# First networks of two tiles side by side, an output product with wide moving operands, and a narrowing without GpSimd

## The chip, the cores and the metric

The kernel runs on one core of one Trainium2 chip. The metric is the device time of one execution in microseconds; three runs of the kernel before gave 1218.34, 1219.1 and 1219.85 us.

## What is computed

For 6016 tokens and 256 channels, a channel attention is followed by two feed-forward networks. Weights come as 64-bit floats and the kernel rounds them to 32 bits itself ("narrowing").

```python
qn, kn = q / norm(q over tokens), k / norm(k over tokens)
a   = softmax(kn.T @ qn / tau)              # 256 x 256
x   = v @ a                                 # 6016 x 256
h   = x @ w_in                              # 2048 wide
g   = h where h >= 1, 0 where h <= -1, (h + 1)**2 / 4 between
y   = g @ w_out                             # first network
xn  = y / sqrt(mean(y*y) + 1e-6) * rms_g
out = (silu(xn @ w_gate) * (xn @ w_val)) @ w_out2   # second network, 1536 wide
```

## The kernel before, in words

Tokens are handled in 12 tiles: eleven of 512 and one of 384. Channels or hidden units lie on the partitions and tokens on the free axis, so that a matmul has a 128x128 stationary block of weights and a moving block of up to 512 tokens. Every product is made from two parts of each operand, a high part rounded to the fp32r format and the remainder: high x high, low x high and high x low, so three matmuls for one. `split` (L88) makes the parts: a copy on ScalarE (L89) and a subtraction (L86), on VectorE or, where an engine is given, on GpSimd.

**Start.** q and k are loaded in 14 chunks (L306 to L336). ScalarE squares them (L320), VectorE sums the squares (L325), TensorE accumulates the 256x256 scores (L298). Norms, softmax and a transpose give `at`, the attention in two parts. It is folded into the first weight: `make_w1` (L411) multiplies a 512-column group of w_in with it, giving w1 in two parts, `w1h` and `w1l`.

**Narrowing.** 34 jobs of 128x512 words narrow the weights. A job loads 512 KB into one of three `wide` buffers (L143) and works in place (`narrow`, L155): VectorE clamps the high words (L158), shifts the three top bits of the low words down (L162), takes the sign bit over (L166); ScalarE scales the exponent (L170); VectorE shifts and joins (L174); ScalarE rounds the high part (L180); GpSimd subtracts (L182). Then the buffer is free for SP's next load. `pump` (L212) moves each of at most two jobs in flight one step on and starts a new one; it is called once for each item of the order, and `require` (L221) calls it until the named weights are ready.

**First network** (A and B). Item ("1", t, f) multiplies w1's block f with tile t's v (`emit_A`, L432, 6 matmuls), makes g (L449, L450 on ScalarE, L451 on VectorE) and splits it (L461: the subtraction is GpSimd's for t < 2 or f < 3). Three items later `emit_B` (L464, 6 matmuls) adds block f's part to the sum y, which has a PSUM buffer of two banks of its own (`ps_y`). After block 15, `norm` (L479) makes the second network's input in five steps on VectorE, ScalarE, GpSimd (the power, L506) and TensorE.

**Second network** (GV and D). Item ("2", t, f) multiplies gate and value block f (`emit_GV`, 12 matmuls), makes u (L552, L553), splits it, and two items later `emit_D` (L564) adds block f's part to the output. There the tokens are the stationary operand, 128 at a time, and the 256 columns of w_out2 move: 12 matmuls of 256 columns in a tile of 512. The output accumulates in a PSUM buffer of its own (`ps_o`), tokens on the partitions; `store` (L580) copies one half on ScalarE (L588) and one on VectorE (L590) and sends each with one DMA of SP.

**Order.** A list written by hand (L597 to L620) holds 16 items of the first network for each tile and, between them, the 12 items of the second network of the tile before, of which six are left for the next tile's time. The scheduler orders the instructions of each engine by a simulated timeline, starting from the order in which they are written. All loads and stores stand on SP's queue.

Of the kernel before, what the change touches and what calls it, by code (L numbers as in the profile page):

```python
# [17 lines left out]
SKEW = 6  # L18
LAG = 12
MID = 8  # L20
# [3 lines left out]
PRE = 2  # L24
# [5 lines left out]
QK_CHUNKS = (2, 2, 4, 4, 4, 4, 4, 4, 4, 4, 4, 3, 2, 2)  # L30

# [4 lines left out]
def tile_channel_attention_two_ffn(  # L36
# [36 lines left out]
    ps_y = ctx.enter_context(tc.tile_pool(name="ps_y", bufs=1, space=bass.MemoryType.PSUM))  # L73
    ps_o = ctx.enter_context(tc.tile_pool(name="ps_o", bufs=1, space=bass.MemoryType.PSUM))

    def mm_tile(name):
        return ps_mm.tile([P, TOK], F32, tag="mm", name=name)

# [76 lines left out]
    def narrow(x, hi, lo):  # L155
# [26 lines left out]
        nc.gpsimd.tensor_tensor(out=lo, in0=got, in1=hi.bitcast(F32), op=ALU.subtract)  # L182
# [4 lines left out]

    later = []
# [5 lines left out]
    def narrow_job():  # L194
        if not wide:
            fetch()
        key, x, dst = wide.pop(0)
        if w1_done[0] >= 0:
            while jobs and len(wide) < STAGE - FLIGHT:
                fetch()  # L200
        hi, lo = dst()
        yield from narrow(x, hi, lo)
        ready.add(key)

    flight = []
    w1_done = [-1]

    def may_start():
        key = wide[0][0] if wide else jobs[0][0] if jobs else None
        return key is not None and not (key[0] == "wi" and key[1] > w1_done[0] + 2)  # L210

    def pump():  # L212
# [33 lines left out]
    def wi_jobs(todo, g):  # L246
        for c in range(NC):
            todo.append((("wi", g, c), (w_in, c * P, 1), g * TOK, wi_dst(g, c)))
# [8 lines left out]
    for g in range(2):  # L257
        wi_jobs(jobs, g)
    wo_jobs(0)
    for g in range(2, NG):  # L260
        wi_jobs(later, g)
        wo_jobs(g - 1)
    wo_jobs(NG - 1)
    w2 = {}
    for g in range(F2 // TOK):
# [20 lines left out]
    s_ps = [  # L286
        ps_y.tile([P, 2, TOK], F32, tag="y", name="s_ps0")[:, 0, :C],
        ps_o.tile([P, 2, 2, C], F32, tag="o", name="s_ps1")[:, 0, 0, :],
    ]
# [47 lines left out]
    for _ in range(PRE):  # L337
        fetch()
# [72 lines left out]
    def make_w1(g, b):  # L411
        h, l = wi[g]
        ah, al = at[b]
        ps = mm_tile(f"w1_ps{g}_{b}")
        i = 0
        for c in range(NC):
            sl = slice(c * P, (c + 1) * P)
            for x, w in ((ah, h), (ah, l), (al, h)):
                nc.tensor.matmul(ps, x[:, sl], w[:, c, :], start=(i == 0), stop=(i == 3 * NC - 1))
                i += 1  # L420
        sl = slice(g * TOK, (g + 1) * TOK)
        split(w1h[:, b, sl], w1l[:, b, sl], ps)
# [33 lines left out]
    def finish_g(t, f):  # L456
# [281 lines left out]
```

## Time and profile before

| what | value |
|---|---|
| median of 3 runs | 1219.1 us (1218.34 to 1219.85) |
| profiled execution | 1220.48 us, span 1218.7 us |
| TensorE busy | 1179.0 us, 97% of the span, 6000 matmuls |
| VectorE busy | 678.5 us, 56% |
| ScalarE busy | 638.3 us, 52% |
| GpSimd busy | 179.8 us, 15% |
| DMA | 43.48 MB, 36 GB/s over the span |

Busy times of engines overlap. A matmul's duration in the profile is longer than the distance to the next one, since matmuls are pipelined; what one costs in a row of them is read from start to start. The idle time of an engine that does not bound the kernel costs nothing. PE is TensorE, DVE VectorE, ACT ScalarE, POOL GpSimd, SPq the queue of SyncE.

### The profile page before, as it was taken

Reading aid. Unit: us, or ns where it says so; the run is one execution under the profiler, and the core shown is the slowest. Engines: PE = TensorE matmul, PEld = TensorE weight load, DVE = VectorE, ACT = ScalarE, POOL = GpSimd, SP = SyncE. Lnnn points to the kernel's source line nnn. Section 1 sums busy time; section 2 is a strip of 40 time slices with the busy share of each in tenths; the row PEclk is TensorE's granted clock in tenths of the full one; section 3 lists DMA queues with packets and bytes.
Section 4 is the critical chain, followed back from the end, with each engine's and each line's share of the span. In section 5 each row is a group of like instructions: output and inputs, shape, how many; then the busy total and the mean of one; then the engine's idle time right before and its main releaser. Section 6 shows DMA issues by size and latency. Waiting matters only on the chain.

```text
span 1218.7 us, 15601 instructions
## 1 busy us (share of the span) xinstructions
PE 1179.0 (97%) x6000; PEld 1010.6 (83%) x6000; DVE 678.5 (56%) x977; ACT 638.3 (52%) x1076; POOL 179.8 (15%) x128
## 2 busy tenths in 40 slices
PE   7888789999999999999999999999999999999998
PEld 6666567888888888888888888888888888899998
DVE  5899999464464464364365355355355345445443
ACT  6566776454464455454455455455445445445432
POOL 0255775110010010010010010010010010010000
PEclk9999899999999999999999999999999999999999
DMA  9734433010001001001001001001001000000000
GB/s 352 191 103 121 116 94 85 1 18 18 1 7 29 1 1 35 1 1 35 1 1 36 1 1 35 1 1 35 1 1 31 1 1 18 1 1 18 1 18 14
DMA packets 67275, 43.48 MB, mean 36 GB/s; under 512 B 51456, under 2 KB 57472, under 8 KB 67200
## 3 DMA queue, kind: packets, MB, share of 16 engines
q1 hardware_dynamic: 67200, 42.48, 12.4%
q8 instruction: 47, 0.77, 0.3%
q14 instruction: 28, 0.23, 0.1%
HBM read 36.31 MB, written 6.16 MB: 35 GB/s over the span
## 4 chain that ended last, share of the span: by engine, by line
PE 84%; DVE 7%; DMA 4%; issue 2%; ACT 1%; SPq 1%; POOL 0%; DVEq 0%; POOLq 0%; ACTq 0%
PE y L471 18%; PE h L439 18%; PE o L573 16%; PE vp L541 15%; PE gp L541 15%; DMA qk<-in_q_dram 2%; DVE wide L162 1%; DVE wide L174 1%; DVE wide L158 1%; DVE wide L166 1%; DVE g L451 1%; DMA wide<-in_moe_w_in_dram 1%; SPq L124 1%; DMA wide<-in_moe_w_out_dram 0%; DMA wide<-in_moe_w_val_dram 0%
## 5 line engine op out<-in xcount | busy, mean ns | idle before, releaser
L89 ACT ACTIVATE uh<-u 128x512 fp32r<-128x512 f32 (+1 forms) x144 | 89.8, 624 | 256.1 <-PE o L573 252.4
L86 POOL TENSOR_TENSOR gl<-g,gh 128x512 fp32r<-128x512 f32 (+1 forms) x62 | 85.6, 1384 | 833.0 <-ACT gh L89 619.8
L451 DVE SCALAR_TENSOR_TENSOR g<-h,g 128x512 f32<-128x512 f32 (+1 forms) x192 | 129.6, 676 | 121.6 <-ACT g L450 121.6
L86 DVE TENSOR_TENSOR ul<-u,uh 128x512 fp32r<-128x512 f32 (+1 forms) x144 | 99.2, 689 | 158.5 <-ACT uh L89 158.0
L553 DVE TENSOR_TENSOR u<-u,vp 128x512 f32<-128x512 f32 (+1 forms) x144 | 97.3, 676 | 136.2 <-PE vp L541 133.7
L89 ACT ACTIVATE gh<-g 128x512 fp32r<-128x512 f32 (+1 forms) x192 | 119.0, 620 | 91.6 <-DVE g L451 90.0
L449 ACT ACTIVATE g<-h 128x512 f32<-128x512 f32 (+1 forms) x192 | 112.5, 586 | 93.7 <-PE h L439 92.5
L573 PE MATMUL o<-wdh,ul 128*128 128x256 f32 x564 | 159.6, 283 | 0.0
L573 PE MATMUL o<-wdl,uh 128*128 128x256 f32 x564 | 159.5, 283 | 0.0
L573 PE MATMUL o<-wdh,uh 128*128 128x256 f32 x564 | 158.8, 282 | 0.0
L439 PE MATMUL h<-vh,w1h 128*128 128x512 f32 (+1 forms) x384 | 150.1, 391 | 8.1 <-DVE g L451 7.8
L471 PE MATMUL y<-gh,woh 128*128 128x512 f32 (+1 forms) x384 | 149.7, 390 | 5.4 <-DVE x L485 4.7
L471 PE MATMUL y<-gl,woh 128*128 128x512 f32 (+1 forms) x384 | 149.8, 390 | 1.9 <-POOL gl L86 1.9
L439 PE MATMUL h<-vh,w1l 128*128 128x512 f32 (+1 forms) x384 | 149.3, 389 | 0.0
L471 PE MATMUL y<-gh,wol 128*128 128x512 f32 (+1 forms) x384 | 149.2, 389 | 0.0
L439 PE MATMUL h<-vl,w1h 128*128 128x512 f32 (+1 forms) x384 | 148.3, 386 | 0.0
L86 DVE TENSOR_TENSOR gl<-g,gh 128x512 fp32r<-128x512 f32 (+1 forms) x130 | 91.1, 701 | 76.5 <-ACT gh L89 75.2
L450 ACT ACTIVATE g<-g 128x512 f32<-128x512 f32 (+1 forms) x192 | 119.0, 620 | 4.4
L541 PE MATMUL gp<-xh,wgh 128*128 128x512 f32 (+1 forms) x288 | 111.7, 388 | 3.8 <-DVE g L451 3.6
L541 PE MATMUL vp<-xh,wvh 128*128 128x512 f32 (+1 forms) x288 | 111.2, 386 | 1.6 <-ACT u L552 1.6
L573 PEld LDWEIGHTS o<-wdl,uh 128*128 128x128 f32 x564 | 107.6, 191 | 5.1
L573 PEld LDWEIGHTS o<-wdh,uh 128*128 128x128 f32 x564 | 107.5, 191 | 5.0
(109 smaller groups left out, 2053.3 us busy)
## 6 DMA issues: line engine op xcount, KB each, us to landing
wide<-in_moe_w_out_dram SPq DMA_DIRECT2D x14, 512.0 KB, 3.7
out_dram<-ob SPq DMA_DIRECT2D x23, 256.0 KB, 2.2
vin<-in_v_dram SPq DMA_DIRECT2D x88, 64.0 KB, 2.5
qk<-in_q_dram SPq DMA_DIRECT2D x9, 512.0 KB, 10.2
qk<-in_k_dram SPq DMA_DIRECT2D x9, 512.0 KB, 10.2
wide<-in_moe_w_in_dram SPq DMA_DIRECT2D x8, 512.0 KB, 4.6
wide<-in_moe_w_gate_dram SPq DMA_DIRECT2D x6, 512.0 KB, 3.6
wide<-in_moe_w_val_dram SPq DMA_DIRECT2D x6, 512.0 KB, 3.6
```

The source lines that it names most:

```text
L86: (eng or nc.vector).tensor_tensor(out=dst_lo, in0=src, in1=hi.bitcast(F32), op=ALU.subtract)
L89: nc.scalar.activation(out=dst_hi, in_=src, func=AF.Copy)
L124: nc.sync.dma_start(out=xv[32 * a:32 * a + 32, c, :n // 32, :], in_=src[a, c])
L158: nc.vector.tensor_scalar(out=high.bitcast(F32), in0=high.bitcast(F32), scalar1=WIDE_MAX, scalar2=-WIDE_MAX, op0=ALU.min, op1=ALU.max,)
L439: nc.tensor.matmul(ps[:, :n], w[:, c, f * P:(f + 1) * P], x[:, c, :n], start=(i == 0), stop=(i == 3 * NC - 1),)
L449: nc.scalar.activation(out=r[:, :n], in_=ps[:, :n], func=AF.Relu, bias=0.5, scale=0.5)
L450: nc.scalar.activation(out=r[:, :n], in_=r[:, :n], func=AF.Square)
L451: nc.vector.scalar_tensor_tensor(out=r[:, :n], in0=ps[:, :n], scalar=1.0, in1=r[:, :n], op0=ALU.max, op1=ALU.min)
L471: nc.tensor.matmul(y_ps[t][:, c, :n], w[:, f, c * P:(c + 1) * P], x[:, :n], start=(f == 0 and i == 0), stop=(f == NF1 - 1 and i == 2),)
L541: nc.tensor.matmul(ps[:, :n], w[:, c, f * P:(f + 1) * P], x[:, c, :n], start=(i == 0), stop=(i == 3 * NC - 1),)
L553: nc.vector.tensor_tensor(out=u[:, :n], in0=u[:, :n], in1=ps[1][:, :n], op=ALU.mult)
L573: nc.tensor.matmul(o_ps[t][:, b // 2, b % 2, :], x[:, sl], w[:, f, :], start=(f == 0 and i == 0 and b % 2 == 0), stop=(f == NF2 - 1 and i ...
```

## The change

- The order is new. The first networks of tiles 0 and 1 run side by side, with tile 1's 16 blocks spread from place 1.5 to 19 along tile 0's; then the first network of tile t has the second network of tile t - 2 beside it. The first four blocks of tile 2 stand alone, and four blocks of tile 0's second network are left for tile 3's time. 24 blocks of the second network follow the last first-network block, where there were 18.
- `y` and the output share two PSUM buffers of two banks (`ps_yo`) in turn.
- `emit_D` makes the weights stationary and the tokens moving, as in B: 6 matmuls of 512 columns for a tile of 512. The output then has channels on the partitions; `store` turns 32x32 blocks on VectorE and sends them with eight DMAs of 64 KB. The last tile keeps the old form.
- In `narrow`, ScalarE makes the low words' three bits by a scaled copy in place of VectorE's shift, and VectorE makes the last subtraction in place of GpSimd.
- g's subtraction is on GpSimd only for t > 3 and f < 3, and the narrowings of w_in write straight to where w1 will stand.
- Ten pumps run beside the q/k chunks 7 to 11 (`PUMPS`); the two loads ahead of time (`PRE`) are gone. A pump is called for every item and a second one for every third.

```diff
-SKEW = 6
-LAG = 12
-MID = 8
+
+
+PAIR = (1.5, 19.0)
+ALONE = 4
+HELD = 4
 BLAG = 3
 W1_AT = (0, 4, 8)
 STAGE = 3
-PRE = 2
...
+PUMPS = (0, 0, 0, 0, 0, 0, 0, 2, 2, 2, 2, 2, 0, 0)
+
+LOW_BITS = 0.9365 * 2.0 ** -29
...
-    ps_y = ctx.enter_context(tc.tile_pool(name="ps_y", bufs=1, space=bass.MemoryType.PSUM))
-    ps_o = ctx.enter_context(tc.tile_pool(name="ps_o", bufs=1, space=bass.MemoryType.PSUM))
+    ps_yo = ctx.enter_context(tc.tile_pool(name="ps_yo", bufs=2, space=bass.MemoryType.PSUM))
...
-        nc.vector.tensor_scalar(
-            out=low, in0=low, scalar1=29, scalar2=None, op0=ALU.logical_shift_right
-        )
+        nc.scalar.activation(out=low, in_=low, func=AF.Copy, scale=LOW_BITS)
         yield
...
-        nc.gpsimd.tensor_tensor(out=lo, in0=got, in1=hi.bitcast(F32), op=ALU.subtract)
+        sub_hi(lo, got, hi)
...
+    wi = {0: [opp.tile([P, NC, TOK], F32R, tag="op", name=f"wi{i}") for i in range(2)]}
+    for g in range(1, F1 // TOK):
+        wi[g] = [w[:, :, g * TOK:(g + 1) * TOK] for w in (w1h, w1l)]
...
+        for _ in range(PUMPS[ci]):
+            pump()
...
-    def make_w1(g, b):
-        h, l = wi[g]
-        ah, al = at[b]
-        ps = mm_tile(f"w1_ps{g}_{b}")
-        i = 0
-        for c in range(NC):
-            sl = slice(c * P, (c + 1) * P)
-            for x, w in ((ah, h), (ah, l), (al, h)):
-                nc.tensor.matmul(ps, x[:, sl], w[:, c, :], start=(i == 0), stop=(i == 3 * NC - 1))
-                i += 1
+    def make_w1(g):
+        require(*[("wi", g, c) for c in range(NC)])
+        h, l = wi.pop(g)
+        got = []
+        for b in range(NC):
+            ah, al = at[b]
+            ps = mm_tile(f"w1_ps{g}_{b}")
+            i = 0
+            for c in range(NC):
+                sl = slice(c * P, (c + 1) * P)
+                for x, w in ((ah, h), (ah, l), (al, h)):
+                    nc.tensor.matmul(
+                        ps, x[:, sl], w[:, c, :], start=(i == 0), stop=(i == 3 * NC - 1)
+                    )
+                    i += 1
+            got.append(ps)
         sl = slice(g * TOK, (g + 1) * TOK)
-        split(w1h[:, b, sl], w1l[:, b, sl], ps)
-        if b == NC - 1:
-            w1_done[0] = g
-            del wi[g]
+        for b in range(NC):
+            split(w1h[:, b, sl], w1l[:, b, sl], got[b])
...
-        split(gh[:, :n], gl[:, :n], r[:, :n], nc.gpsimd if t < 2 or f < 3 else nc.vector)
+        split(gh[:, :n], gl[:, :n], r[:, :n], nc.gpsimd if t > 3 and f < 3 else nc.vector)
...
-            y_ps[t] = ps_y.tile([P, 2, TOK], F32, tag="y", name=f"y{t}")
+            y_ps[t] = yo_tile(f"y{t}")
...
+            o_ps[t] = yo_tile(f"o{t}")
         uh, ul = u_op.pop((t, f))
         wdh, wdl = w2["dh"], w2["dl"]
-        for b in range(n // P):
-            sl = slice(b * P, (b + 1) * P)
-            for i, (x, w) in enumerate(((uh, wdh), (uh, wdl), (ul, wdh))):
+        if t == NT - 1:
+
+            for b in range(n // P):
+                sl = slice(b * P, (b + 1) * P)
+                o = o_ps[t][:, b // 2, (b % 2) * C:(b % 2 + 1) * C]
+                for i, (x, w) in enumerate(((uh, wdh), (uh, wdl), (ul, wdh))):
+                    nc.tensor.matmul(
+                        o, x[:, sl], w[:, f, :],
+                        start=(f == 0 and i == 0 and b % 2 == 0),
+                        stop=(f == NF2 - 1 and i == 2),
+                        skip_group_check=True,
+                    )
+            return
+        for c in range(NC):
+            sl = slice(c * P, (c + 1) * P)
+            for i, (w, x) in enumerate(((wdh, uh), (wdl, uh), (wdh, ul))):
                 nc.tensor.matmul(
-                    o_ps[t][:, b // 2, b % 2, :], x[:, sl], w[:, f, :],
-                    start=(f == 0 and i == 0 and b % 2 == 0),
-                    stop=(f == NF2 - 1 and i == 2),
-                    skip_group_check=True,
+                    o_ps[t][:, c, :n], w[:, f, sl], x[:, :n],
+                    start=(f == 0 and i == 0), stop=(f == NF2 - 1 and i == 2),
...
+        if t < NT - 1:
+            dst = out[n0:n0 + n, :].rearrange("(b j) (c a i) -> a c j b i", j=32, c=NC, a=4, i=32)
+            for c in range(NC):
+                ob = tmp_tile(f"ob{t}_{c}")
+                nc.vector.transpose(out=ob[:, :n], in_=o[:, c, :n])
+                src = ob.rearrange("p (b i) -> p b i", i=32)
+                for a in range(4):
+                    nc.sync.dma_start(out=dst[a, c], in_=src[32 * a:32 * a + 32, :n // 32, :])
+            return
...
+    at_block = [((f, 0), ("1", 0, f)) for f in range(NF1)]
+    for f in range(NF1):
+        at_block.append(((PAIR[0] + f * (PAIR[1] - PAIR[0]) / (NF1 - 1), 1), ("1", 1, f)))
+    order = [block for _, block in sorted(at_block)]
+
+    second = [("2", t, f) for t in range(NT) for f in range(NF2)]
+    done = 0
+    for t in range(2, NT):
+        first = ALONE if t == 2 else 0
+        n = NF2 - HELD if t == 2 else NF2 + HELD if t == 3 else NF2
+        base = done
         for f in range(NF1):
             order.append(("1", t, f))
-            if f < mid:
-                keep = len(early) * (mid - 1 - f) // mid
-                if early:
-                    keep = min(keep, SKEW * (mid - 1 - f) // mid)
-                while len(early) > keep:
-                    order.append(early.pop(0))
-            else:
-                keep = (NF2 - SKEW) * (NF1 - 1 - f) // (NF1 - mid)
-                while len(late) > keep:
-                    order.append(late.pop(0))
-    order.append(("flush1",))
-    order += m2
-    order += [("2", NT - 1, f) for f in range(NF2)]
+            while done < base + n * (f + 1 - first) // (NF1 - first):
+                order.append(second[done])
+                done += 1
+    order += [("B",)] * BLAG
+    order += second[done:]
...
+        work(1)
+        pump()
+        if i % 3 == 0:
             pump()
```

## Rows read from the trace of the kernel before

**Rows 1.** Windows of three stretches: length, busy us (instructions) by engine, PEclk, DMA share, GB/s.

```profile
64.60:204.20 139.60, 115.77 (x471) 88.42 (x470) 136.57 (x173) 98.31 (x172) 89.63 (x60) 0.95 0.40 111
204.20:1214.70 1010.50, 1010.48 (x5308) 877.85 (x5307) 495.93 (x747) 501.14 (x853) 81.61 (x57) 1.00 0.05 11
257.19:351.37 94.18, 94.18 (x483) 80.67 (x483) 46.60 (x70) 47.85 (x81) 7.32 (x5) 1.00 0.05 12
```

**Rows 2.** Timeline of TensorE from 500 us: start us, duration us, line, operation.

```profile
500.40 0.28 PE L573 MATMUL o<-wdh,uh 128*128 128x256 f32 x1
...
501.83 0.40 PE L439 MATMUL h<-vh,w1h 128*128 128x512 f32 x1
...
503.22 0.39 PE L471 MATMUL y<-gh,woh 128*128 128x512 f32 x1
...
504.58 0.39 PE L541 MATMUL gp<-xh,wgh 128*128 128x512 f32 x1
```

**Rows 3.** Groups of TensorE from 64.6 to 204.2 us: count, busy us, mean ns.

```profile
L573 PE MATMUL o<-wdl,uh 128*128 128x256 f32 x9 | 2.5, 283 | 0.0
L573 PE MATMUL o<-wdh,uh 128*128 128x256 f32 x9 | 2.5, 282 | 0.0
L573 PE MATMUL o<-wdh,ul 128*128 128x256 f32 x8 | 2.3, 283 | 0.0
```

**Rows 4.** Groups of VectorE in the same stretch.

```profile
L166 DVE SCALAR_TENSOR_TENSOR wide<-wide 128x512 uint32<-128x512 uint32 x28 | 29.5, 1053 | 0.2
L174 DVE SCALAR_TENSOR_TENSOR wide<-wide 128x512 uint32<-128x512 uint32 x28 | 28.0, 1002 | 0.7 <-ACT wide L170 0.6
L162 DVE TENSOR_SCALAR wide<-wide 128x512 uint32<-128x512 uint32 x27 | 22.3, 827 | 0.0
L158 DVE TENSOR_SCALAR wide<-wide 128x512 f32<-128x512 f32 x27 | 21.9, 813 | 2.1 <-DMA wide<-in_moe_w_in_dram 0.9 <-DMA wide<-in_moe_w_out_dram 0.6 <-DMA wide<-in_moe_w_val_dram 0.5
L451 DVE SCALAR_TENSOR_TENSOR g<-h,g 128x512 f32<-128x512 f32 x31 | 20.7, 676 | 0.0
```

**Rows 5.** Timeline of all engines from 85 us: start us, duration us.

```profile
86.49 0.68 DVE L451 SCALAR_TENSOR_TENSOR g<-h,g 128x512 f32<-128x512 f32 x1
...
87.09 0.68 DVE L166 SCALAR_TENSOR_TENSOR wide<-wide 128x512 uint32<-128x512 uint32 x1
...
90.94 1.50 POOL L182 TENSOR_TENSOR wol<-wide,woh 128x512 fp32r<-128x512 f32 x1
...
91.18 1.53 DVE L162 TENSOR_SCALAR wide<-wide 128x512 uint32<-128x512 uint32 x1
...
93.96 0.42 DVE L158 TENSOR_SCALAR wide<-wide 128x512 f32<-128x512 f32 x1
...
94.30 0.42 DVE L162 TENSOR_SCALAR wide<-wide 128x512 uint32<-128x512 uint32 x1
...
94.63 0.69 DVE L86 TENSOR_TENSOR w1l<-w_ps,w1h 128x512 fp32r<-128x512 f32 x1
```

**Rows 6.** Groups of VectorE in the whole span: count, busy us, mean ns.

```profile
L325 DVE TENSOR_TENSOR acc<-acc,sq 128x2048 f32<-128x2048 f32 x9 | 20.6, 2293 | 13.4 <-ACT sq L320 13.4
...
L500 DVE STREAM_TRANSPOSE sb<-ms 128x512 f32<-128x512 f32 x11 | 7.8, 706 | 1.3 <-PE ms L499 1.3
...
L590 DVE COPY ob<-o 128x512 f32<-128x512 f32 x11 | 7.5, 685 | 0.0
```

**Rows 7.** Timeline of ScalarE, five instructions in a row from 153.28 us.

```profile
153.28 0.58 ACT L449 ACTIVATE g<-h 128x512 f32<-128x512 f32 x1
153.76 0.66 ACT L170 ACTIVATE wide<-wide 128x512 f32<-128x512 f32 x1
...
155.41 0.57 ACT L449 ACTIVATE g<-h 128x512 f32<-128x512 f32 x1
```

**Rows 8.** Timeline of SP's queue at the end of the q/k stage.

```profile
28.15 8.82 SPq L124 DMA_DIRECT2D vin<-in_v_dram  x5
37.08 0.42 SPq L310 DMA_DIRECT2D qk<-in_q_dram  x1
```

More of the change, by code (lines that the diff above doesn't have):

```diff
@@ L186, in tile_channel_attention_two_ffn @@
     ready = set()
-    later = []
     def fetch():
@@ L197, in narrow_job @@
         key, x, dst = wide.pop(0)
-        if w1_done[0] >= 0:
-            while jobs and len(wide) < STAGE - FLIGHT:
-                fetch()
+        while jobs and len(wide) < STAGE - FLIGHT:
+            fetch()
         hi, lo = dst()
@@ L215, in pump @@
                 flight.remove(job)
-        if len(flight) < FLIGHT and may_start():
+        if len(flight) < FLIGHT and (wide or jobs):
             job = narrow_job()
@@ L256, in tile_channel_attention_two_ffn @@
     NG = F1 // TOK
[L257 to L263, printed above, removed]
+    later = []
+    for g in range(NG):
+        wi_jobs(g)
+        wo_jobs(g)
     w2 = {}
@@ L285, in tile_channel_attention_two_ffn @@
     acc = sp.tile([P, 2, JM, C], F32, name="acc")
[L286 to L289, printed above, removed]
+    s_ps = [yo_tile(f"s_ps{b}")[:, 0, :C] for b in range(NC)]
     NQ = len(QK_CHUNKS)
@@ L630, in work, with finish_all_g, next_B @@
                 tasks.remove(task)
[L632 to L637 removed]
+                n_norms[0] = max(0, n_norms[0] - 1)
     m1, m2 = [], []
+    def finish_all_g():
+        for key in list(g_f32):
+            finish_g(*key)
     def step1(t, f):
         if t == 0 and f in W1_AT:
[L642 to L645 removed]
+            make_w1(W1_AT.index(f) + 1)
         ps = emit_A(t, f)
         m1.append((t, f))
[L648 to L649 removed]
+        finish_all_g()
         start_g(t, f, ps)
         if len(m1) > BLAG:
[L652 to L654 removed]
+            next_B()
+    def next_B():
+        t, f = m1.pop(0)
+        if (t, f) in g_f32:
+            finish_all_g()
         if t == 0:
@@ L658, in did_B @@
         if f == NF1 - 1:
-            tasks.insert(0, norm(t))
+            n_norms[0] += 1
+            tasks.insert(n_norms[0] - 1, norm(t))
     def step2(t, f):
@@ L677, in did_D @@
             store(t)
-    for it in order:
+    jobs.extend(later)
+    for _ in v0:
+        pass
+    make_w1(0)
+    for i, it in enumerate(order):
         if it[0] == "1":
             _, t, f = it
-            if f == 0 and t + 1 < NT:
+            if t == 0 and f == 1:
+                load_v(1)
+                for _ in prep_v(1):
+                    pass
+            if t > 0 and f == 0 and t + 1 < NT:
                 load_v(t + 1)
-            if f == 8 and t + 1 < NT:
+            if t > 0 and f == 8 and t + 1 < NT:
                 tasks.append(prep_v(t + 1))
             step1(t, f)
-            work(1)
-            pump()
         elif it[0] == "2":
@@ L692, in tile_channel_attention_two_ffn @@
             step2(*it[1:])
-            work(1)
-            pump()
-        else:
-            finish_g(*m1[-1])
-            for i in range(BLAG, 0, -1):
-                did_B(*m1[-i])
-            work(2)
+        else:
+            next_B()
+        work(1)
+        pump()
+        if i % 3 == 0:
+            pump()
     finish_u(*m2[-1])
```

48 lines of the change are left out of this document (9 added, 39 removed).

## The prediction, made blind

> **What bounds the kernel now.** I read the stretches first [rows 1]. From 204.2 us to 1214.7 us TensorE is busy for 1010.48 of 1010.50 us at full granted clock, with VectorE and ScalarE at half load: here only less TensorE work can shorten the time. One tile takes 94.18 us there, again without a gap. The stretch before it, from the first matmul of tile 0's first network (64.6 us) to 204.2 us, looks different: VectorE is busy 136.57 of 139.6 us, ScalarE 98.31, and TensorE holds only 471 matmuls. So there are two questions: what do the second part's matmuls cost, and what does VectorE do in the first.
>
> For the matmuls the timeline of TensorE by single instructions serves, read from start to start, since the durations overlap [rows 2]. Twelve 256-column matmuls of emit_D take 501.83 - 500.40 = 1.43 us, 0.119 each. Six 512-column ones of emit_B take 504.58 - 503.22 = 1.36 us, 0.2267 each. Twice 0.119 is 0.238, so a split matmul costs about 12 ns more than a whole one of the same columns. The six of emit_A that stand right behind emit_D take 1.39 us, 0.2317 each: 0.03 us per block more.
>
> In the stretch at the start, 26 of the 471 matmuls are those short ones [rows 3]; the work is 445 x 0.2267 + 26 x 0.119 = 104.0 us, and 139.6 - 104.0 = 35.6 us are lost. The cause is VectorE: the four narrowing groups (L158, L162, L166, L174) make 101.7 of its 136.57 us [rows 4]. In the timeline [rows 5] L162 runs 1.53 us while GpSimd's subtraction of 1.50 us runs, and 0.42 us when none does; L162 and L166 have means of 0.827 and 1.053 us against 0.42 and 0.68 for single free ones. GpSimd's subtractions stretch VectorE. Free instructions start 0.60 us apart (86.49 to 87.09) and the two of 0.42 us 0.34 apart (93.96, 94.30, 94.63).
>
> **The change, part by part.** The sum is made against the profiled execution: 1220.48 us, span 1218.7. The median of three runs is 1219.1, 1.4 us below; I take the differences from the median.
>
> *emit_D with 512 columns.* For 11 of 12 tiles, six matmuls take the place of twelve in each of 132 blocks. A whole tile then has 96 + 96 + 144 + 72 + 2 = 410 matmuls of 512 columns, 410 x 0.2267 = 92.95 us, against 94.18 [rows 1]: 1.23 us, in 11 tiles 13.5 us. Of this 0.03 x 132 = 4.0 us is the slower pitch behind emit_D; if it stays, 9.5. I take 13.5, since emit_D becomes like emit_B, behind which the pitch is 0.2267; it is all on the path, as nothing hides TensorE there. Ends: 9.5 and 13.5.
> The Trainium skill (TensorE: Matmul & The Clock Gate, Back-to-back issue gap) gives a lone warm matmul N/2.4 + 2.5 ns, so a removed matmul of the same total columns would save 2.5 ns; 792 of them give an estimate of 2.0 us. The rows here show 0.119 and 0.2267 us where that formula has 0.109 and 0.216, and I go by the rows.
>
> *The store.* Two 32x32-block transposes on VectorE take the place of a ScalarE copy and a VectorE copy (0.685 us); from PSUM such a transpose takes 0.706 [rows 6]. That is 0.73 us more per tile on an engine busy 46.60 of 94.18 us [rows 1]: free. Eight DMAs of 64 KB stand on SP's queue instead of two, in front of later v loads, which have a tile's time. The last tile keeps the old form, so the end is as now. The output buffer is free only after both transposes, and the sum of one tile and the output of another now take turns in two buffers. Waiting for them is the first block of the next emit_D, with one or two blocks of TensorE work (2.7 us each) in between; if VectorE comes late, up to 0.5 us in each of ten turns, 5 us. Ends 0 and 5; I take 1.5.
>
> *Narrowing and gl on VectorE, the bits on ScalarE.* Without GpSimd's subtractions a narrowing costs VectorE 0.34 (clamp) + 3 x 0.60 = 2.14 us. The subtraction has no row on VectorE; between 0.34 and L166's 1.053 I take 0.60, as a free two-operand one in rows 5. ScalarE gets a third instruction; its integer conversion has no row: between 0.58 (L449) and L166's 1.053, I take L170's kind, 0.66 [rows 7]. From the first matmul of tile 0 to the first block of the second network the new order has 32 first-network blocks of the pair and 6 of tile 2, all but about four and a half of the 34 narrowings (ten pumps now run beside the q/k chunks), three pairs of w1 splits, v for tiles 1 and 2, and one norm with the start of another.
> VectorE: 75 for the blocks, 6, 8, 11 + 4, and 28 x 4 + 5 = 117 for narrowing: 221, of which 29 clamps: 192 x 0.60 + 29 x 0.34 = 125 us. ScalarE: 114, 87, 6, 4 and 7, 218 at the pitch of rows 7 ((155.41 - 153.28) / 4 = 0.53): 116 us. TensorE: 38 x 6 + 35 x 6 + 36 + 4 = 478 matmuls, 108.4 us. So VectorE still bounds the stretch, with ScalarE close behind it, and not the 139.6 us of now. It may start some 3 us of this before the first matmul. Now its busy share is 136.57 / 139.6 = 0.98; two nearly full engines that hand work to each other four times per narrowing will not keep that, and I take 0.93: 122 / 0.93 = 131 us. Lost on TensorE: 131 - 108.4 = 22.6 in place of 35.6, a gain of 13.0 us. Ends: VectorE fully packed, 122 us (gain 22); 0.85, 144 us (no gain). What is late next is the subtraction behind ScalarE's third copy, which also frees a wide buffer for SP's next load.
>
> *Narrowing beside q and k.* Up to seven wide loads of 512 KB enter SP's queue among the q/k loads, where three were. SP can be held: five v loads from 28.15 us took 8.82 us and the next q load went out at 37.08 [rows 8]. VectorE's additions there take 2.293 us each [rows 6], and it gets four whole and two begun narrowings (10 us) where it had three of two-thirds (6 us). The first matmul of tile 0 moves by 0 to 4 us; I take +1.5. That w1 is ready earlier is no gain of its own: it is in the stretch.
>
> Sum: -13.5 - 13.0 + 1.5 + 1.5 = -23.5; 1219.1 - 23.5 = 1195.6, rounded to **1196 us**.
>
> **Rivals.** *No gain at the start*: the queues of ScalarE and VectorE wait for each other and the stretch takes 144 us (VectorE's share 0.85). For it: ScalarE goes from 98 us of work to 116 in a shorter time, and 34 narrowings are placed ahead of the second network. Against: the lock by GpSimd is gone. 1219.1 - 13.5 + 3 = 1208.6 us.
> *Short matmuls are no dearer than their columns*: the pitch of 0.119 comes from something that the longer ones keep. Then emit_D gains 2 us: 1196 + 11.5 = 1207.5. Against: the two pitches of rows 2 differ by one fixed term.
> *Better*: a good part of the narrowing fits before 64.6 us or behind the first second-network blocks, so that the stretch takes 115 us: 1219.1 - 13.5 - 29 + 3 = 1179.6.
> *Slower*: the hand-offs cost much more than 0.93. Place: the same stretch, all 34 narrowings in front of the second network while TensorE's queue stands behind wo's narrowing at the first emit_B. Price: 122 / share - 108.4. It decides from a share of 0.79, where the stretch is 154 us and loses 46 us, the 35.6 of now and the 10.5 left of the other parts; at 0.76 it is 160 us, and the time 1225. Against: now VectorE has 0.98.
>
> **How the numbers follow.** Forecast 0.55, no gain at the start 0.20, short matmuls no dearer 0.05, better 0.12, slower 0.08. The forecast's own ends: 1219.1 - 13.5 - 22 = 1183.6, with the start fully packed and nothing lost elsewhere, and 1219.1 - 9.5 - 6 + 4 + 5 = 1212.6, with under half of the gain at the start and the upper ends of the rest. The range 1182 to 1213 leaves out the slower case and most of the better one, together just under 0.2. A difference of 0.2% (2.4 us) is about what a measurement of this kernel can tell. Faster by more: 0.91; within: 0.03; slower: 0.06, the slower case less its part close to the point.
>
> **What would show it.** One tile of the middle takes 92.9 us instead of 94.2, with emit_D at 0.227 per matmul and the blocks behind it too. L158, L166 and L174 have means of 0.42, 0.69 and 0.69 us. The first second-network matmul starts about 131 us behind the first emit_A, which stands near 66 us; behind it TensorE has no gaps but short ones at the turns of the output buffer. I am wrong if emit_D's block still takes 1.43 us, if ScalarE's new copy takes over 1 us, if the first emit_A stands beyond 70 us, or if VectorE is idle for over 15% of the stretch.

## The result and the profile after

The changed kernel takes 1198.57 us, the median of four runs (1197.09 to 1199.66), against 1218.89 before: ratio 0.9832, interval 0.9815 to 0.9849. It is 20.3 us faster, and the forecast was 1196. Its profiled execution is the fastest of the four, 1197.09 us with a span of 1193.7 (3.4 us lie outside, 1.8 before), so the two spans differ by 25.0 us. The windows below split those 25.0 us; the medians say 20.3. Of the 4.7 us between the two, 1.5 are that low execution (1197.09 against 1198.57), 1.6 the profiled execution of the kernel before, which was a high one (1220.48 against 1218.89), and 1.6 what lies outside the spans. In the experiment no_pumps below the profiled execution was disturbed (5658 us), so it has three times and no stretch is read from it. Line numbers are those of each kernel's own text.

Windows of the changed kernel, columns as in [rows 1]: from the first emit_A (L432) to the first second-network matmul (L534), the stretch without gaps behind it, and one window of 92.95 us in the middle:

```profile
74.10:194.90 120.80, 110.69 (x473) 88.89 (x471) 113.30 (x198) 110.12 (x204) 3.13 (x2) 0.99 0.38 112
...
204.40:1189.70 985.30, 985.14 (x4468) 826.62 (x4468) 487.96 (x747) 488.22 (x819) 63.96 (x46) 1.00 0.07 11
300.00:392.95 92.95, 92.95 (x412) 76.93 (x411) 42.26 (x63) 45.30 (x75) 6.97 (x5) 1.00 0.08 12
```

92.95 us of the middle hold 412 matmuls without a gap, those cut by the window's ends counted; a tile has 410 and took 94.18 us before [rows 1]. The 985 us of the middle hold 0.16 us without a matmul. The stretch at the start is 120.8 us long instead of 139.6. Its 473 matmuls of 0.2267 us are 107.2, so 13.6 us are lost in place of 35.6. But it begins at 74.1 us instead of 64.6, and that gives nearly half of it back.

PEclk, the granted clock of TensorE as a share of its upper level (2.4 GHz), is 0.95 on average in the stretch before and 0.99 now. As an estimate from these two rows, 0.05 x 139.6 = 7.0 us of full-speed TensorE time were withheld before and 1.2 now, so up to 5.8 of the 22.0 us could be the clock's; no run separates that. Against much of it: narrow_only below shortens the stretch by 16.5 us with the same matmuls at a PEclk of 0.94, and in softmax_first, at 0.95, VectorE's share of the stretch is the same 0.94 as here.

Timeline of TensorE, to hold against [rows 2]:

```profile
508.53 0.39 PE L579 MATMUL o<-uh,wdh 128*128 128x512 f32 x1
...
509.89 0.39 PE L432 MATMUL h<-vh,w1h 128*128 128x512 f32 x1
...
511.25 0.39 PE L464 MATMUL y<-gh,woh 128*128 128x512 f32 x1
```

emit_D's six take 1.36 us instead of 1.43, and the six of emit_A behind them 1.36 instead of 1.39: the slower pitch is gone too.

One whole tile, read from its norm's matmul to that of the next tile, first in the kernel before and then in the changed one:

```profile
338.37 0.39 PE L498 MATMUL ms<-sh,ones_r 128*128 128x512 f32 x1
432.56 0.39 PE L498 MATMUL ms<-sh,ones_r 128*128 128x512 f32 x1
...
478.80 0.39 PE L491 MATMUL ms<-sh,ones_r 128*128 128x512 f32 x1
571.78 0.39 PE L491 MATMUL ms<-sh,ones_r 128*128 128x512 f32 x1
```

It takes 92.98 us instead of 94.19, with 72 matmuls fewer.

Groups of VectorE and then of ScalarE in 74.1 to 194.9 us (count, busy us, mean ns, idle us before and what ended it), to hold against [rows 4]:

```profile
L444 DVE SCALAR_TENSOR_TENSOR g<-h,g 128x512 f32<-128x512 f32 x38 | 25.7, 681 | 3.3 <-ACT g L443 3.2
L93 DVE TENSOR_TENSOR gl<-g,gh 128x512 fp32r<-128x512 f32 x37 | 25.1, 682 | 0.5 <-ACT gh L96 0.4
L171 DVE SCALAR_TENSOR_TENSOR wide<-wide 128x512 uint32<-128x512 uint32 x25 | 17.0, 683 | 0.3 <-ACT wide L169 0.3
L179 DVE SCALAR_TENSOR_TENSOR wide<-wide 128x512 uint32<-128x512 uint32 x25 | 17.0, 682 | 0.1
L165 DVE TENSOR_SCALAR wide<-wide 128x512 f32<-128x512 f32 x24 | 10.0, 421 | 2.7 <-DMA wide<-in_moe_w_out_dram 2.6
...
L169 ACT ACTIVATE wide<-wide 128x512 uint32<-128x512 uint32 x24 | 16.4, 684 | 5.4 <-DMA wide<-in_moe_w_out_dram 2.6 <-DMA wide<-in_moe_w_val_dram 1.2 <-DVE g L444 0.7
```

Every VectorE instruction of the narrowing has its free duration now (L166 had 1.053 us, its successor L171 has 0.683). ScalarE's new copy, L169, takes 0.684. Only 25 of the 34 narrowings lie in the stretch; the others were made ahead of it, and there they cost something.

Timeline of VectorE, ScalarE and TensorE around the softmax of the changed kernel:

```profile
50.23 1.33 DVE L165 TENSOR_SCALAR wide<-wide 128x512 f32<-128x512 f32 x1 [1.09 <-DMA wide<-in_moe_w_in_dram]
...
52.09 1.36 DVE L357 TENSOR_SCALAR rq<-rq 128x256 f32<-128x256 f32 x1
...
54.44 1.74 DVE L358 RECIPROCAL rq<-rq 128x256 f32<-128x256 f32 x1
...
56.11 0.62 DVE L179 SCALAR_TENSOR_TENSOR wide<-wide 128x512 uint32<-128x512 uint32 x1
56.65 0.67 DVE L171 SCALAR_TENSOR_TENSOR wide<-wide 128x512 uint32<-128x512 uint32 x1
...
60.70 1.28 ACT L372 ACT_TABLE_LOAD   x1
62.00 0.51 ACT L372 ACTIVATE s_sb<-s_sb,mx 128x256 f32<-128x256 f32 x1
...
63.88 0.66 PE L380 MATMUL a_ps<-ident,s_sb 128*128 128x128 f32 x2 [12.50 <-DVE s_sb L377]
...
65.99 0.70 ACT L169 ACTIVATE wide<-wide 128x512 uint32<-128x512 uint32 x1 [0.90 <-DMA wide<-in_moe_w_in_dram]
...
66.59 0.63 ACT L96 ACTIVATE ah<-a_ps 128x256 fp32r<-128x256 f32 x2
...
74.11 0.39 PE L432 MATMUL h<-vh,w1h 128*128 128x512 f32 x1
```

The same steps of the kernel before:

```profile
51.22 1.75 DVE L369 RECIPROCAL rq<-rq 128x256 f32<-128x256 f32 x1
51.96 1.28 ACT L383 ACT_TABLE_LOAD   x1
...
55.14 0.51 ACT L383 ACTIVATE s_sb<-s_sb,mx 128x256 f32<-128x256 f32 x1 [1.89 <-DVE mx L382]
...
56.66 1.25 PE L391 MATMUL a_ps<-ident,s_sb 128*128 128x128 f32 x4 [4.11 <-DVE sm L386]
...
57.35 0.38 ACT L89 ACTIVATE ah<-a_ps 128x256 fp32r<-128x256 f32 x1 [1.12 <-PE a_ps L391]
...
64.61 0.39 PE L439 MATMUL h<-vh,w1h 128*128 128x512 f32 x1
```

Narrowing steps (L165, L171, L179) now stand between the softmax's instructions, on VectorE and ScalarE, and some of them wait for a load while the softmax stands behind them in the queue. The transposed scores (a_ps) come 7.2 us later (63.88 against 56.66), and the copy behind them (ah) follows after 2.7 us instead of 0.7, because narrowing steps stand ahead of it on ScalarE, among them L169 at 65.99, which waited 0.90 us for a load. 7.2 + 2.0 makes 9.2 of the 9.5 us by which the first emit_A is late. Part of the 7.2 us is the table load in front of the exponential (1.28 us): before, ScalarE made it at 51.96 us, while it waited for VectorE's maximum (mx); now it comes at 60.70, behind ScalarE's narrowing copies, and the exponential waits for it.

So the spans' 25.0 us are: -13.5 for emit_D, -22.0 for the stretch, +9.5 for its later begin, together -26.0; 1.0 us is left over for all else.

### The profile page after: what moved, and what is told of

Read it like the earlier page. It is cut to its first block, busy times and chain, and to the rows that moved or that the text cites. A ratio compares the mean times of both kernels' runs of the same rounds, so it can differ in the third digit from the quotient of the medians.

```text
span 1193.7 us, 13953 instructions
## 1 busy us (share of the span) xinstructions
PE 1159.3 (97%) x5208; PEld 968.0 (81%) x5208; DVE 663.2 (56%) x1026; ACT 652.5 (55%) x1099; POOL 70.9 (6%) x56
## 3 DMA queue, kind: packets, MB, share of 16 engines
q1 hardware_dynamic: 107680, 42.48, 14.3%
## 4 chain that ended last, share of the span: by engine, by line
PE 87%; ACT 4%; DMA 4%; DVE 3%; issue 1%; SPq 0%; ACTq 0%; DVEq 0%
PE h L432 19%; PE y L464 19%; PE gp L534 16%; PE vp L534 16%; PE o L579 15%; DMA wide<-in_moe_w_in_dram 2%; PE o L569 1%; ACT g L442 1%; DMA qk<-in_q_dram 1%; ACT wide L175 1%; ACT gh L96 1%; DMA wide<-in_moe_w_out_dram 1%; ACT g L443 1%; ACT sq L309 0%; PE w_ps L411 0%
## 5 line engine op out<-in xcount | busy, mean ns | idle before, releaser
L432 PE MATMUL h<-vh,w1h 128*128 128x512 f32 (+1 forms) x384 | 148.7, 387 | 5.1 <-DVE g L444 2.8
L93 DVE TENSOR_TENSOR gl<-g,gh 128x512 fp32r<-128x512 f32 (+1 forms) x168 | 113.5, 677 | 65.0 <-ACT gh L96 63.2
L432 PE MATMUL h<-vh,w1l 128*128 128x512 f32 (+1 forms) x384 | 148.4, 386 | 1.1 <-DVE w1l L93 1.1
L432 PE MATMUL h<-vl,w1h 128*128 128x512 f32 (+1 forms) x384 | 148.1, 386 | 0.0
L464 PE MATMUL y<-gl,woh 128*128 128x512 f32 (+1 forms) x384 | 147.3, 385 | 0.0
L534 PE MATMUL gp<-xh,wgh 128*128 128x512 f32 (+1 forms) x288 | 110.9, 385 | 1.4 <-ACT xh L96 1.4
L534 PE MATMUL gp<-xh,wgl 128*128 128x512 f32 (+1 forms) x288 | 110.9, 385 | 0.0
L534 PE MATMUL vp<-xh,wvh 128*128 128x512 f32 (+1 forms) x288 | 110.8, 385 | 0.0
L534 PE MATMUL vp<-xh,wvl 128*128 128x512 f32 (+1 forms) x288 | 110.8, 385 | 0.0
L534 PE MATMUL vp<-xl,wvh 128*128 128x512 f32 (+1 forms) x288 | 110.8, 385 | 0.0
L534 PE MATMUL gp<-xl,wgh 128*128 128x512 f32 (+1 forms) x288 | 110.7, 385 | 0.0
L545 ACT ACTIVATE u<-gp 128x512 f32<-128x512 f32 (+1 forms) x144 | 84.9, 589 | 45.8 <-PE gp L534 28.7
L579 PE MATMUL o<-ul,wdh 128*128 128x512 f32 x264 | 102.9, 390 | 0.0
```

The lines of the kernel that those rows point to most:

```text
L93: (eng or nc.vector).tensor_tensor(out=dst_lo, in0=src, in1=hi.bitcast(F32), op=ALU.subtract)
L432: nc.tensor.matmul(ps[:, :n], w[:, c, f * P:(f + 1) * P], x[:, c, :n], start=(i == 0), stop=(i == 3 * NC - 1),)
L464: nc.tensor.matmul(y_ps[t][:, c, :n], w[:, f, c * P:(c + 1) * P], x[:, :n], start=(f == 0 and i == 0), stop=(f == NF1 - 1 and i == 2),)
L534: nc.tensor.matmul(ps[:, :n], w[:, c, f * P:(f + 1) * P], x[:, c, :n], start=(i == 0), stop=(i == 3 * NC - 1),)
L545: nc.scalar.activation(out=u[:, :n], in_=ps[0][:, :n], func=AF.Silu)
L579: nc.tensor.matmul(o_ps[t][:, c, :n], w[:, f, sl], x[:, :n], start=(f == 0 and i == 0), stop=(f == NF2 - 1 and i == 2),)
```

## The experiments

All times are medians of four runs (no_pumps: three); the kernel before took 1219.12 us beside the first four kernels and 1220.39 beside the others. "From" names the kernel that an edit starts from.

| run | from | us | ratio to before (interval) |
|---|---|---|---|
| wide_d_only | before | 1208.06 | 0.9902 (0.9887 to 0.9917) |
| narrow_only | before | 1205.28 | 0.9881 (0.9861 to 0.9900) |
| old_order | before | 1193.88 | 0.9784 (0.9770 to 0.9799) |
| cap4 | changed | 1198.60 | 0.9823 (0.9804 to 0.9841) |
| softmax_first | changed | 1189.27 | 0.9739 (0.9722 to 0.9755) |
| old_softmax_first | old_order | 1188.27 | 0.9732 (0.9717 to 0.9746) |
| no_pumps | changed | 1201.07 | 0.9842 (0.9826 to 0.9859) |
| sub_gpsimd | changed | 1199.71 | 0.9830 (0.9815 to 0.9845) |
| sf_gl_gpsimd | softmax_first | 1202.96 | 0.9851 (0.9834 to 0.9868) |
| sf_sub_gpsimd | softmax_first | 1202.30 | 0.9842 (0.9820 to 0.9864) |
| sf_both_gpsimd | softmax_first | 1203.35 | 0.9852 (0.9832 to 0.9873) |
| sf_shift_vector | softmax_first | 1197.41 | 0.9810 (0.9786 to 0.9833) |

**emit_D alone.** The kernel before with the diff's emit_D and store, in an output buffer of its own:

```diff
-    o_ps[t] = ps_o.tile([P, 2, 2, C], F32, tag="o", name=f"o{t}")
+    o_ps[t] = ps_o.tile([P, 2, TOK], F32, tag="o", name=f"o{t}")
...
+            for i, (w, x) in enumerate(((wdh, uh), (wdl, uh), (wdh, ul))):
+                nc.tensor.matmul(o_ps[t][:, c, :n], w[:, f, sl], x[:, :n], ...
```

> The kernel before with the 512-column emit_D and its store alone, the output in its own PSUM buffer. If a matmul costs its columns plus a fixed term of about 13 ns, one tile of the middle takes 92.95 us instead of 94.18 and the time falls by 13.5 us to 1205.4. If a removed matmul saves only 2.5 ns, as the formula for a lone matmul has it, the tile takes 94.0 us and the time is 1217. The first emit_A stays at 64.6 us and the stretch behind it as it was.

The medians differ by 11.1 us and the spans by 13.5 (1205.2 against 1218.7). The first emit_A did not stay at 64.6 us; it comes 1.2 us earlier, for a reason that was not looked into. Without that, 12.3 of the 13.5 us are left for emit_D. The first emit_A and the window in the middle:

```profile
63.45 0.50 PE L439 MATMUL h<-vh,w1h 128*128 128x512 f32 x1 [1.05 <-DVE w1l L86]
...
300.00:392.95 92.95, 92.95 (x412) 76.94 (x411) 47.05 (x70) 47.23 (x79) 7.32 (x5) 1.00 0.08 12
```

The term holds, with 11 to 12.3 us. The 2 us that the formula cited in the prediction gives (the Trainium skill, TensorE: Matmul & The Clock Gate, Back-to-back issue gap) are not what this kernel shows: a tile takes 1.21 us less with 72 matmuls fewer, so a removed matmul saved 17 ns, 12 of it by its own pitch ((1.43 - 1.36) / 6) and 5 by the slower pitch behind emit_D that went with it (0.03 us a block).

**Narrowing alone.** The kernel before, its order kept, with the bits on ScalarE and the subtractions on VectorE:

```diff
-        nc.vector.tensor_scalar(out=low, in0=low, scalar1=29, ..., op0=ALU.logical_shift_right)
+        nc.scalar.activation(out=low, in_=low, func=AF.Copy, scale=0.9365 * 2.0 ** -29)
-        nc.gpsimd.tensor_tensor(out=lo, in0=got, in1=hi.bitcast(F32), op=ALU.subtract)
+        sub_hi(lo, got, hi)
-    split(gh[:, :n], gl[:, :n], r[:, :n], nc.gpsimd if t < 2 or f < 3 else nc.vector)
+    split(gh[:, :n], gl[:, :n], r[:, :n], nc.gpsimd if t > 3 and f < 3 else nc.vector)
```

> The kernel before, its order kept, with the bits on ScalarE, the narrowing's subtraction on VectorE and g's subtraction on GpSimd only for t over 3. If GpSimd's subtractions held VectorE up, L158 and L166 fall to 0.42 and 0.69 us, VectorE's 136.6 us of the stretch to about 110, and with 0.93 of it busy the stretch takes some 118 us: about 20 us off, 1199. If the gain at the start needs the pair of first networks (tile 0 alone leaves TensorE waiting for the next weights), the means fall all the same but the time by under 8 us: above 1211.

13.8 us faster. Its window from the first emit_A to the point behind which TensorE has no gap, and its groups of VectorE from 64 to 200 us:

```profile
66.90:190.00 123.10, 112.91 (x471) 89.25 (x471) 111.61 (x194) 105.29 (x191) 3.48 (x2) 0.94 0.43 119
...
L172 DVE SCALAR_TENSOR_TENSOR wide<-wide 128x512 uint32<-128x512 uint32 x28 | 19.1, 686 | 0.8 <-ACT wide L168 0.8
L164 DVE SCALAR_TENSOR_TENSOR wide<-wide 128x512 uint32<-128x512 uint32 x28 | 19.0, 685 | 0.7 <-ACT wide L162 0.7
...
L158 DVE TENSOR_SCALAR wide<-wide 128x512 f32<-128x512 f32 x28 | 11.9, 425 | 6.2 <-DMA wide<-in_moe_w_in_dram 2.4 <-DMA wide<-in_moe_w_val_dram 1.6 <-DMA wide<-in_moe_w_gate_dram 1.1
```

With the same 471 matmuls the stretch takes 123.1 us instead of 139.6, 16.5 less; the first emit_A stands 2.3 us later. That is less than the 20 us expected: VectorE has the 111.6 us of work that was expected (110), but a share of 0.91 instead of 0.93, and the later start was not counted. Moving the work between engines is enough to free VectorE; the new order is not needed for it.

**Both, in the old order.** The two edits above together: everything of the change but its order of blocks, its shared output buffers, the pumps beside q and k with their new beat, and the new place where w_in is narrowed to.

> The kernel before, its order kept, with both: wide emit_D and store, and the narrowing on ScalarE and VectorE. If the two parts are apart in time they add: 13.5 and what the run with the narrowing alone gives, so 1186 where that gives 20. It tells what the new order and the pumps beside q and k are worth: if the new order is needed, this stays above the changed kernel's 1198.6 by some 10 us; if its late first emit_A (74 us in place of 65) is a loss, it is below.

-25.2 us, and the two alone make -11.1 - 13.8 = -24.9: they add up. It is below the changed kernel by 4.7 us, with intervals that do not meet. The first emit_A stands at 66.3 us here. So the order, the shared buffers, the pumps and the new place, as they are, are no part of the gain: together they cost some 5 us. Against narrow_only, emit_D gives 11.4 us here.

**Fewer narrowings before the attention is done.** The changed kernel, which may begin only four of them until then, with two loads ahead of time (not shown in the diff):

```diff
-        if len(flight) < FLIGHT and (wide or jobs):
+        if len(flight) < FLIGHT and (wide or jobs) and started[0] < cap[0]:
+            started[0] += 1
...
+    cap[0] = 34
     jobs.extend(later)
```

> The changed kernel, but no more than four narrowings are started until the attention is done; two more loads are made ahead of time. If the steps of the fifth to seventh narrowing in the queues of VectorE and ScalarE, some waiting for late loads, are what holds the softmax up, the first emit_A comes at about 67 us instead of 74.1 and the time falls by 4 to 7 us, to 1192 to 1195. If the work is only put off, the stretch behind it grows by as much (three narrowings, 2.1 us each, and the wait for them at the first emit_B), and the time stays within 2 us of 1198.6.

No change, and the first emit_A even later, at 77.8 us. Two instructions of VectorE from its softmax:

```profile
65.67 0.69 DVE L171 SCALAR_TENSOR_TENSOR wide<-wide 128x512 uint32<-128x512 uint32 x1
66.28 0.35 DVE L383 TENSOR_SCALAR s_sb<-s_sb,sm 128x256 f32<-128x256 f32 x1
```

The edit did not do what it was meant to: the steps that it moved behind the softmax in the program text stand among the softmax's instructions in the queues all the same. The order in the queues is the scheduler's, and it draws ahead what does not depend on the softmax. The theory is not tested by this run.

**Narrowings held behind the softmax.** The changed kernel with a cap of 3, the two loads of cap4, and the next four narrowings queued behind the softmax's last multiplication and the last copy of its result. `issue_after` makes what is written inside it stand behind the given instruction in that engine's queue:

```diff
+    def step(job):
+        with ExitStack() as held:
+            if anchors and 3 <= job[0] < 7:
+                for a in anchors:
+                    held.enter_context(tc.issue_after(a))
+            return next(job[1], "end")
...
+    anchors += [last_mul.ins, last_copy.ins]
```

> The changed kernel with three narrowings beside q and k, and the fourth to seventh queued on VectorE and ScalarE behind the softmax's last multiplication and copy. The run with the cap alone did not take their steps out of the softmax: the scheduler drew them forward. If these steps and the loads that they wait for are what puts the first emit_A at 74 us, it comes at 64 to 66 us now. Four narrowings (2.1 us of VectorE each) then fall into the stretch behind it, so of the 8 to 10 us some 3 to 5 stay: 1193 to 1196. If all of it is paid back in the stretch, the time stays at 1198.6 within 2 us, and the first emit_A is early all the same.

9.3 us below the changed kernel, more than expected. The softmax of this kernel in the timeline, and the window from its first emit_A to its first second-network matmul:

```profile
48.88 1.20 DVE L374 TENSOR_SCALAR rq<-rq 128x256 f32<-128x256 f32 x1 [0.38 <-ACT rq L370]
...
50.11 1.75 DVE L375 RECIPROCAL rq<-rq 128x256 f32<-128x256 f32 x1
...
53.45 0.51 ACT L389 ACTIVATE s_sb<-s_sb,mx 128x256 f32<-128x256 f32 x1 [2.72 <-DVE mx L388]
...
54.97 1.25 PE L399 MATMUL a_ps<-ident,s_sb 128*128 128x128 f32 x4 [3.12 <-DVE sm L392]
...
55.38 1.09 DVE L165 TENSOR_SCALAR wide<-wide 128x512 f32<-128x512 f32 x3
```

```profile
61.70:189.60 127.90, 116.58 (x484) 92.70 (x483) 120.49 (x211) 116.62 (x213) 3.48 (x2) 0.95 0.42 124
```

The held narrowings (L165 at 55.38) begin behind the softmax, a_ps comes 8.9 us earlier than in the changed kernel and the first emit_A 12.4 us earlier. The stretch is 7.1 us longer, as VectorE has 7 us more work in it; its share is 0.94 in both kernels, though PEclk is 0.95 here and 0.99 there. That nets -5.3 us of a span difference of -6.0; the medians differ by more, since the profiled execution of the changed kernel was its lowest. cap4, with the same two loads and a cap of 4, left the first emit_A late. So softmax_first shows that the narrowings in the softmax caused the late start, and that the work costs less behind the softmax than inside it.

**The same in the old order.** The hold, put into old_order:

> The kernel before, its order kept, with wide emit_D and the narrowing on ScalarE and VectorE (1193.9), and the fourth to seventh narrowing queued behind the softmax. Its first emit_A stood at 66.3 us, with one step waiting 1.36 us for a load within the softmax. If that is what it lost against the kernel before (64.6), it gains 1 to 2 us: 1192 to 1193. If the later start of these narrowings counts more, it is 1194 or above.

The fastest kernel of the study, 5.6 us below old_order and 10.3 below the changed kernel. The gain is not where it was sought: the first emit_A stands at 67.1 us, not earlier than 66.3. Windows up to 185 us, of old_order:

```profile
66.30:185.00 118.70, 105.33 (x431) 82.16 (x430) 106.98 (x186) 101.42 (x184) 3.48 (x2) 0.96 0.41 115
```

and of old_softmax_first:

```profile
67.10:185.00 117.90, 109.56 (x462) 86.13 (x461) 110.68 (x194) 105.30 (x192) 3.54 (x2) 0.99 0.40 116
```

Thirty-one more matmuls fit into 0.8 us less. From 67 to 185 us the bits on ScalarE (L162) waited 14.3 us in old_order and 8.4 here, most of it for loads. Why the loads come in time here was not separated, and stays open. The clock differs too, 0.96 against 0.99 in the two rows: by the estimate used above 4.7 and 1.2 us withheld, so up to 3.5 us of the gain may be the clock's.

**No narrowing beside q and k.** `PUMPS` all zero, two loads ahead of the v loads instead:

> The changed kernel with no narrowing placed beside q and k, two loads ahead of time as before. If the pumps beside q and k are what delays the attention, the first emit_A comes at 66 us or so, as in the run of both parts with the old order, and four narrowings more fall into the stretch behind it, 8.6 us of VectorE: the time stays within 2 us of 1198.6. If the delay comes from the requests that follow the softmax in the text, the first emit_A stays at 72 to 75 us, and the time is some 5 us worse.

The runs took 1201.03 to 1202.33 us; where the first emit_A stood isn't known. The interval overlaps with the changed kernel's: the pumps are worth a few us at most. The order of VectorE's queue can be read: between the first step on rq and the last multiplication (L359 to L379) stand five narrowing steps, where the changed kernel has eleven (L357 to L377). Leaving out the pumps thins them out and does not clear them.

**The narrowing's subtraction back on GpSimd**, in the changed kernel:

```diff
-        sub_hi(lo, got, hi)
+        sub_hi(lo, got, hi, nc.gpsimd)
```

> The changed kernel with the narrowing's last subtraction back on GpSimd, 34 of them, nothing else. VectorE has 34 x 0.60 = 20 us less to do. If each subtraction of 1.4 us holds one instruction of VectorE for about 1 us, its means rise again (L165 from 0.45 towards 0.7, L171 and L179 from 0.68 towards 0.95), VectorE gains nothing net or loses some 10 us, and the time is 1199 to 1209. If the lock does not matter, VectorE is 20 us lighter, ScalarE bounds the stretch, and the time falls to 1194 or below.

```profile
71.60:200.10 128.50, 117.71 (x477) 90.72 (x477) 115.99 (x175) 112.33 (x204) 43.79 (x29) 0.96 0.39 110
```

No measurable difference in the medians. In the stretch the means rise (L165 421 to 601 ns, L171 683 to 742, L179 682 to 805), and it is 128.5 us instead of 120.8, but the first emit_A stands at 71.6 instead of 74.1. Less VectorE work in the softmax may be what pays for that part. The late start of the changed kernel hides part of what the subtractions are worth, so the four last runs start from softmax_first.

**gl back on GpSimd** (the condition `t < 2 or f < 3` of before):

> The run with the softmax first (1189.3; its first emit_A stands steadily, so the stretch of 127.9 us can be compared), with g's subtraction back on GpSimd for t under 2 or f under 3; the narrowing stays on VectorE. VectorE loses 37 instructions of 0.60 us in the stretch. If GpSimd's lock is worth more than the work, L171 and L179 rise from 0.68 to 0.85 or more, and with g's part 1.4 us late instead of 0.7 the time is 1192 to 1200. If only the count of VectorE's work matters, the stretch shortens to ScalarE's 116 us and the time falls to 1180 or so.

```profile
61.90:202.10 140.20, 122.69 (x475) 91.88 (x473) 126.04 (x175) 115.87 (x212) 54.89 (x37) 0.94 0.39 113
```

+13.7 us. 140.2 - 475 x 0.2267 = 32.5 us are lost in the stretch, against 127.9 - 484 x 0.2267 = 18.2 in softmax_first: the whole loss is there. It is more than the 1192 to 1200 us expected where the lock outweighs the work.

**The narrowing's subtraction back on GpSimd:**

> The run with the softmax first, with the narrowing's subtraction back on GpSimd alone. On the changed kernel this gave back by the lock 12 us of the 20 that VectorE shed, and left the time as it was. If the two cancel, 1189 to 1193; if the lock is worth more, above 1194.

```profile
63.30:198.00 134.70, 117.25 (x477) 89.76 (x475) 118.56 (x183) 117.64 (x213) 51.13 (x33) 0.97 0.41 118
```

+13.0 us, though VectorE sheds 28 subtractions. 26.6 us are lost, 8.4 more than in softmax_first, and the first emit_A is 1.6 us later. The profiled execution was the lowest of the four (1198.62 us), so the spans differ by 9.1 us only.

**Both back:**

> The run with the softmax first, with both subtractions back on GpSimd, 37 and about 30 of some 1.45 us in the stretch, so that GpSimd is busy for 100 of 128 us, as before. If the lock grows with GpSimd's busy share, L171 and L179 return towards 1.0 us and L165 to 0.8, and the stretch grows to 140 us or so: 1199 to 1207, more than the two single edits together. If the lock is no cause, VectorE has 40 us less to do and the time is 1180.

```profile
63.30:198.10 134.80, 115.80 (x465) 87.21 (x464) 114.79 (x140) 113.40 (x206) 99.20 (x66) 0.96 0.43 117
...
L171 DVE SCALAR_TENSOR_TENSOR wide<-wide 128x512 uint32<-128x512 uint32 x27 | 28.9, 1072 | 0.3
L179 DVE SCALAR_TENSOR_TENSOR wide<-wide 128x512 uint32<-128x512 uint32 x27 | 25.8, 957 | 2.1 <-ACT wide L175 1.8
L165 DVE TENSOR_SCALAR wide<-wide 128x512 f32<-128x512 f32 x27 | 25.1, 929 | 12.1 <-DMA wide<-in_moe_w_out_dram 5.2 <-DMA wide<-in_moe_w_val_dram 2.8 <-DMA wide<-in_moe_w_gate_dram 2.1
```

+14.1 us, hardly more than either alone and not the sum of the two that was expected. 134.8 - 465 x 0.2267 = 29.4 us are lost, 11.2 more than in softmax_first. The means are near those of [rows 4] again (L166 1.053, L174 1.002, L158 0.813). Undoing it brings back the stretched instructions, so GpSimd's subtractions were their cause; but either half alone pays nearly the whole price.

**The three bits back on VectorE** (the shift of before in place of ScalarE's copy):

> The run with the softmax first, with the low words' bits made by VectorE's shift again. VectorE gets 30 x 0.34 = 10 us more in the stretch, ScalarE 30 x 0.53 = 16 us less. If VectorE bounds the stretch, it grows by 8 to 10 us and the time is 1197 to 1200. If the two engines bound it together, by waiting for each other, the shorter chain on ScalarE gives as much back and the time stays within 3 us of 1189.3.

```profile
64.00:197.40 133.40, 119.80 (x489) 94.69 (x488) 127.41 (x235) 102.67 (x183) 3.80 (x2) 0.95 0.40 115
```

+8.1 us. ScalarE's work falls from 116.6 to 102.7 us and VectorE's rises from 120.5 to 127.4: VectorE bounds the stretch; 13.9 us less on ScalarE bought nothing. The stretch is 5.5 us longer, and the first emit_A 2.3 us later.

## Why the prediction was right, and where it was off

**The bound** was read rightly. VectorE's stretched instructions made the start slow, and the matmul count the rest: one edit on each gives 11 and 14 us, and they add up.

**emit_D** was predicted at 13.5 us. By itself it is worth 11.1 us in the medians and 12.3 in the spans, where the earlier first emit_A of that run is left out. For one tile the working was right: 92.98 us, with the slower pitch gone. Over the whole kernel it gives one to two us less than the sum for eleven tiles; where the difference goes was not traced.

**The store** was priced at +1.5 us (0 to 5) for turns of the output buffer. The whole middle has 0.16 us without a matmul, so the term is about nothing: the one or two blocks in between cover it.

**The first emit_A** is the step that failed: "The first matmul of tile 0 moves by 0 to 4 us; I take +1.5." It moved by 9.5 to 74.1 us, beyond the 70 us that the prediction itself had named as a sign of being wrong. I had counted the narrowings that enter SP's queue and VectorE's work beside q and k, but not that they would go on between the steps of the softmax, which is a chain in which each step waits for the last. softmax_first shows it by taking them out: there the first emit_A stands at 61.7 us.

**The stretch** was taken as 131 us and is 120.8; its gain is 22.0 us instead of 13.0. The share was right: 113.30 / 120.8 = 0.94, where 0.93 stood. The instructions were not: "all but about four and a half of the 34 narrowings" is 25 in place of 29.5, so that VectorE has 198 instructions with 113 us instead of 221 with 125 (122 of them behind the first matmul). [rows 4] could have warned of it: with 27 of 34 clamps in its stretch and one behind, the kernel before had begun six narrowings ahead of its first emit_A, and ten pumps more could hardly leave 4.5. Per instruction the estimate held: 125 / 221 = 0.566 us forecast, 113.30 / 198 = 0.572 measured. ScalarE's new copy, taken at 0.66, has 0.684. The whole loss of 35.6 us was put down to VectorE; that PEclk was 0.95 in that row, and part of the loss perhaps the clock's, is not in the prediction.

The two errors belong together. The four and a half narrowings missing from the stretch, at 2.14 us each 9.6 us of VectorE, are those that stand ahead of the first emit_A. +8.0 on one side of 74.1 us and -9.0 on the other cancel, and the total came out 2.6 us from the forecast. The right total is therefore no proof of its two terms.

**The rivals.** *No gain at the start* and *slower* needed VectorE's share to fall to 0.85 and 0.79; it is 0.94. *Short matmuls are no dearer* falls with wide_d_only. *Better* got its shorter stretch (115 forecast, 120.8 measured) but not its time, since the late start was not in its sum; softmax_first at 1189 got part of that gain, by an early first emit_A and with a stretch of 127.9 us.

The order of the blocks was priced only through counts. old_order shows that it gives nothing here; with the hold, the two orders are 1 us apart (1189.27 and 1188.27, with intervals that overlap).

## What to carry to other kernels

Price an engine that bounds a stretch by its free durations and its count of instructions, and check that count on both sides of the stretch's begin: work that leaves it goes somewhere. Before independent work is moved up, look at what latency chain it will be queued in; a queue that runs in order makes the chain wait for that work's loads too, and writing it later in the program does not keep it out where a scheduler orders the queues. Holding four narrowings behind the softmax was worth 9.3 us in the medians, nearly half of what the whole change gained.

## What the runs showed of the hardware

A fixed part of some 12 ns per matmul shows in the pitches: 0.119 us at 256 columns against 0.2267 at 512. The slower pitch of a 512-column block (0.2317 us) behind 256-column ones vanishes with them. Together they make the 1.21 us that a tile takes less with 72 matmuls fewer.

What GpSimd's subtractions cost VectorE is not additive: 13.7 us for one group of them, 13.0 for the other, 14.1 for both, while L171's mean goes from 0.683 us to 0.918, 0.762 and 1.072. The narrowing's subtractions cost nearly as much as gl's with a much smaller rise of the means. In both runs the clamp (L165) waited longer for what it needs from the loads, 9.6 us with gl's subtractions on GpSimd and 11.7 with the narrowing's, against 4.6 in softmax_first, so late loads may be part of both prices; this was not tested by itself.

ScalarE's conversion of 512 columns of uint32 takes 0.684 us, no longer than its copies to fp32r beside it (L185, 0.681).
